# An mLSTM and bilinear kernel: the low words' top bits made on ACT instead of DVE, from the sixth weight stage on

## The chip, the cores and the metric

The kernel runs on one core of a Trainium2 chip. Its time is device time in microseconds (us), median of several runs. Engines are named as the profile names them: PE (matmul) and PEld (its weight loads), DVE, ACT, POOL, and SP, which here only issues DMAs.

## The reference

Inputs are float64. First a gated linear attention over 768 steps, for 4 batches and 8 heads of width 40:

```python
for t in range(S):
    m_new = np.maximum(f_gate[:, :, t] + m, i_gate[:, :, t])
    f_stab = np.exp(f_gate[:, :, t] + m - m_new)
    i_stab = np.exp(i_gate[:, :, t] - m_new)
    m = m_new
    C = f_stab[..., None, None] * C + i_stab[..., None, None] * np.einsum('bhd,bhe->bhde', vt, kt)
    n = f_stab[..., None] * n + i_stab[..., None] * kt
    h_tilde = np.einsum('bhde,bhe->bhd', C, qt)
    nq = np.einsum('bhd,bhd->bh', n, qt)[:, :, None]
    y[:, :, t] = sigmoid(o_gate[:, :, t]) * h_tilde / np.maximum(np.abs(nq), 1.0)
```

Then a bilinear layer on the 3072 tokens x 320 features: `out = ((x @ w_a) * (x @ w_b)) @ w_out`, with an inner width of 1536.

## The kernel before, in words

**Chunks and blocks.** A chunk is 128 steps of one batch (24 chunks, 8 heads each). Two or three chunks make a block of tokens (nine blocks; the first two have two chunks, 256 columns). For each block the bilinear layer (`moe_block`) runs over 12 slices ff of 128 inner columns: `up(ff)` makes two PSUM tiles pu (16 matmuls), ACT copies the first to g, DVE multiplies the second into it, ACT rounds the product to gh, POOL (later DVE) makes the rest gl, and two slices later `down(ff)` multiplies gh and gl with w_out into pd. While a block runs, the attention of the following chunks is woven in (`run_block`).

**Weights.** The weights come as 64-bit words by DMA (`fetch`, raw tiles), in 32 stages of 128 rows by 384 or 320 columns: for each three ff slices four stages of w_a and w_b, one that holds the last 64 rows of both, and three of w_out. Each stage is turned into float32 and split in two parts for PE:
- `high` (L342, ACT): the words' high halves, rescaled, go to a buffer `step` (four of them, in the qks tiles).
- `low` (L349, DVE): the words' low halves, as unsigned integers times 2^-29 and at most 7: the top three bits, into a buffer cw (four of them).
- `join` (L354, DVE): the high part shifted left by three, or'ed with the low bits, in cw.
- `lead_part` (L367, ACT): cw rounded to the leading part of w. `low_part` (L373, DVE): the rest.

Stages 0 to 4 are written out by hand in the opening. Stages 5 to 31 come from `weights()`, one step at each fourth PE instruction of block 0.

**Order.** The opening is in written order. In blocks 0 and 1 a list scheduler orders the instructions of every engine by its own timeline and costs; from block 2 on only ACT, DVE and POOL are ordered by it, PE and SP by hand. Each engine executes its queue strictly in the order built.

**Gates.** `later_gates` makes the decay tables: scans on DVE (L218, L228), a DMA to g_dram (L235) and back as gbc (L180), transposes on PE (ptg), an Exp on ACT into gtab (L263). From gtab POOL makes vw = v times its weight (L854), one buffer for all chunks, and PE's state update pU (L544) needs vw. POOL also masks gbc (L406) once the DMA has brought it back. `begin_e` makes the decay matrix of chunks 2 and 3 on PE (pE, in the same three PSUM buffers as pu) and ACT (Exp, L784). ACT's Exp and Sigmoid are in different tables, so that an ACT_TABLE_LOAD stands wherever they alternate.

Of the kernel before, what the change touches and what calls it, by code (L numbers as in the profile page):

```python
# [12 lines left out]
U32 = mybir.dt.uint32  # L13
I64 = mybir.dt.int64
AF = mybir.ActivationFunctionType
ALU = mybir.AluOpType
# [4 lines left out]
def kernel(  # L21
# [13 lines left out]
    nc = tc.nc  # L35
# [63 lines left out]
    x = ident[0:BH, 0:BH].rearrange("k (x j) -> k x j", j=2)  # L99
# [211 lines left out]
    NF0 = 5  # L311
# [25 lines left out]
    def high(x):  # L337
        raw, n, W = held[x]
        if W is None:
            held[x][2] = cpool.tile([P, WCH], F32, tag="cv", name="cw", bufs=CVB)[:, :n]  # L340
        hi = raw.bitcast(F32).rearrange("p (n w) -> p n w", w=2)[:, :, 1]
        nc.scalar.activation(  # L342
            step[x % len(step)][:, :n], hi, AF.Prelu, scale=2.0 ** -112, alpha=-(2.0 ** 32)
        )

    def low(x):
        raw, n, W = held[x]
        lo = raw.bitcast(U32).rearrange("p (n w) -> p n w", w=2)[:, :, 0]
        nc.vector.tensor_scalar(W.bitcast(U32), lo, 2.0 ** -29, 7.0, op0=ALU.mult, op1=ALU.min)  # L349

    def join(x):
        raw, n, W = held[x]
        wu, tu = W.bitcast(U32), step[x % len(step)][:, :n].bitcast(U32)
        nc.vector.scalar_tensor_tensor(  # L354
            wu, tu, 3, wu, op0=ALU.logical_shift_left, op1=ALU.bitwise_or
        )
# [6 lines left out]
    def lead_part(x):  # L363
        raw, n, W = held[x]
        w = ws[x] = rpool.tile([P, 2, n], F32R, tag=f"s{x}", name=f"w{x}")
        for rows, other, j, jl in parts(x):
            after["act"] = nc.scalar.copy(w[rows, j], W[rows]).ins  # L367

    def low_part(x):
        raw, n, W = held.pop(x)  # L370
        w = ws[x]
        for rows, other, j, jl in parts(x):
            after["dve"] = nc.vector.tensor_tensor(  # L373
                w[other, jl], W[rows], w[rows, j].bitcast(F32), op=ALU.subtract
            ).ins

    def weights():
        for x in range(NF0, len(stages) + 1):
            if x < len(stages):
                with tc.issue_after(start["act"]):  # L380
                    high(x)
                with tc.issue_after(start["dve"]):
                    low(x)
                join(x)
                yield x
            if x > NF0:
                ready[0] = x
                lead_part(x - 1)
                low_part(x - 1)
                yield x  # L390
        for x in qks2:
            for w in range(2):
                nc.gpsimd.memset(x[:, w, :, 3 * D:], 0.0)
# [502 lines left out]
    with tc.manual_schedule(engines={mybir.EngineType[x] for x in ("PE", "Activation", "DVE", "SP")}):  # L896
# [40 lines left out]
        high(0)  # L937
        run(E[0], 2)
        low(0)
        join(0)  # L940
        lead_part(0)
# [6 lines left out]
        run(S_[1])  # L948
        high(2)
        low(2)  # L950
        join(2)
        lead_part(2)
# [36 lines left out]
        for g in (*A, *E, *S_, *V, *F, *X):  # L989
            assert next(g, "end") == "end"  # L990
    conv = weights()

    def rest():
# [73 lines left out]
```

## Time and profile before

| | |
|---|---|
| median of 3 runs | 566.85 us (566.21 to 568.91) |
| profiled execution | 564.22 us, span 562.4 us |
| PE busy | 534.6 us, 95% of the span |
| DVE, ACT, POOL busy | 411.9, 221.3, 126.6 us |
| last weight stage done (L373) | 88.9 us after the span's start |

A row of a timeline gives start, duration, engine, line, operation, tiles and how many instructions it merges; in brackets stands the idle time of the engine before it and what ended it. Rows that follow each other closely overlap by about 0.1 us. A row of groups gives busy time and mean ns of one. PEclk is the clock that PE was granted.

### The profile page before, as it was taken

The page shows a single profiled execution, that of the slowest core. Times are in us where ns is not written, and L with a number is a line of the kernel's source. Part 1 is how long each engine was busy: PE and PEld are TensorE (multiplying, and loading weights), DVE is VectorE, ACT ScalarE, POOL GpSimd, SP SyncE. Part 2 cuts the span into 40 slices and gives each one's busy share as a digit, 9 for nine tenths or more (in the row PEclk, how much of TensorE's full clock was granted, in tenths as well). Part 3 has the DMA queues.
Part 4 walks back from the last instruction along what each step waited for, and adds up shares of the span by engine and source line. Part 5 has one row for each costly group of instructions (what it writes and reads, how often), then busy time and mean ns, then how long its engine had stood idle before and what let it go on. Part 6 is the DMA issues. An engine that isn't in the chain of part 4 may idle for free.

```text
span 562.4 us, 12436 instructions
## 1 busy us (share of the span) xinstructions
PE 534.6 (95%) x4810; PEld 505.9 (90%) x4810; DVE 411.9 (73%) x967; ACT 221.3 (39%) x530; POOL 126.6 (23%) x185
## 2 busy tenths in 40 slices
PE   9678799997999999999999999999999999899997
PEld 6576699997999989999899999899999999799997
DVE  6899976468879965978859995978859577744342
ACT  5677854344422642332632441541432515111111
POOL 2012245253331230332132231233030202100000
PEclk9587789999999999999999999999999999999999
DMA  9999513567956955677855654967544834200001
GB/s 172 300 273 303 110 38 89 117 95 160 153 135 105 167 119 76 146 142 158 139 119 119 120 108 106 190 121 155 89 122 75 139 76 114 35 1 24 2 0 36
DMA packets 198679, 66.77 MB, mean 119 GB/s; under 512 B 184252, under 2 KB 191900, under 8 KB 198620
## 3 DMA queue, kind: packets, MB, share of 16 engines
q1 hardware_dynamic: 198620, 65.98, 57.8%
q8 instruction: 38, 0.62, 0.5%
q14 instruction: 21, 0.17, 0.1%
HBM read 41.11 MB, written 5.97 MB: 84 GB/s over the span
## 4 chain that ended last, share of the span: by engine, by line
PE 68%; DVE 5%; DMA 5%; issue 4%; ACT 3%; SPq 2%; POOL 1%; POOLq 0%; ACTq 0%; DVEq 0%
PE pu L744 39%; PE pd L716 18%; PE pV L520 3%; PE pS L468 2%; PE pU L544 2%; DMA osig<-in_o_gate_dram 1%; ACT gbc L413 1%; PE pX L630 1%; PE pS L818 1%; PE pI L494 1%; PE pV L870 1%; DMA T<-qks 1%; SPq L160 1%; DMA gbc<-g_dram 1%; DMA qk<-in_q_dram 1%
## 5 line engine op out<-in xcount | busy, mean ns | idle before, releaser
L744 PE MATMUL pu<-xh,w 128*128 128x384 f32 (+1 forms) x1080 | 282.5, 328 | 3.9 <-DVE w L373 2.2
L744 PE MATMUL pu<-xl,w 128*128 128x384 f32 (+1 forms) x648 | 210.7, 327 | 1.0 <-DVE xl L636 1.0
L744 PEld LDWEIGHTS pu<-xh,w 128*128 128x128 f32 x1080 | 194.1, 192 | 7.1 <-DVE w L373 3.4
L716 PE MATMUL pd<-w,gh 128*128 128x320 f32 x576 | 132.8, 315 | 1.0 <-ACT gh L754 1.0
L744 PEld LDWEIGHTS pu<-xl,w 128*128 128x128 f32 x648 | 124.7, 193 | 2.0 <-DVE xl L636 1.3
L716 PEld LDWEIGHTS pd<-w,gh 128*128 128x128 f32 x576 | 97.9, 190 | 1.6 <-ACT gh L754 1.2
L752 DVE TENSOR_TENSOR g<-pu,g 128x384 f32<-128x384 f32 (+1 forms) x108 | 54.6, 505 | 56.7 <-PE pu L744 53.7
L716 PE MATMUL pd<-w,gl 128*128 128x320 f32 x288 | 89.2, 315 | 0.0
L751 ACT COPY g<-pu 128x384 f32<-128x384 f32 (+1 forms) x92 | 40.5, 440 | 114.4 <-PE pu L744 114.1
L413 ACT ACTIVATE gbc<-gbc,gtab 128x128 f32<-128x128 f32 x160 | 49.4, 389 | 23.8 <-POOL gbc L406 23.8
L455 POOL TENSOR_TENSOR vr<-va 128x336 f32<-128x336 f32 x18 | 14.0, 775 | 187.1 <-PE pV L520 176.6
L716 PEld LDWEIGHTS pd<-w,gl 128*128 128x128 f32 x288 | 53.8, 189 | 0.0
L756 DVE TENSOR_TENSOR gl<-g,gh 128x384 fp32r<-128x384 f32 (+1 forms) x92 | 50.3, 546 | 1.6
L754 DVE CAST gh<-g 128x384 fp32r<-128x384 f32 (+1 forms) x96 | 32.7, 341 | 1.6
L475 ACT CAST pb<-gbc 128x512 bf16<-128x512 f32 x36 | 22.2, 616 | 26.7 <-DVE gbc L473 26.6
L527 DVE TENSOR_TENSOR num<-pV,num 128x336 f32<-128x336 f32 x18 | 9.1, 504 | 29.9 <-PE pV L520 29.9
L406 POOL TENSOR_SCALAR_AFFINE_SELECT gbc<-gbc 128x1024 f32<-128x1024 f32 x20 | 23.7, 1185 | 18.9 <-DMA gbc<-g_dram 17.1
L562 ACT CAST cb<-cst 128x168 bf16<-128x168 f32 x18 | 6.0, 331 | 54.6 <-DMA gbc<-g_dram 26.7
L473 DVE TENSOR_TENSOR gbc<-pS,gbc 128x512 f32<-128x512 f32 x36 | 24.5, 680 | 3.6 <-PE pS L468 3.6
L520 PEld LDWEIGHTS <-pb 128*128 128x128 bf16 x576 | 23.1, 96 | 4.2 <-DVE pb L479 1.8
L607 POOL TENSOR_TENSOR osig<-osig,den 128x320 f32<-128x320 f32 x22 | 17.0, 771 | 43.8 <-DVE den L602 25.4
L431 ACT CAST qks<-qk 128x320 bf16<-128x320 f32 x36 | 16.1, 452 | 27.3 <-DMA T<-qks 12.4
(130 smaller groups left out, 814.1 us busy)
## 6 DMA issues: line engine op xcount, KB each, us to landing
gbc<-g_dram SPq DMA_DIRECT2D x20, 512.0 KB
qk<-in_q_dram SPq DMA_DIRECT2D x24, 160.0 KB
qk<-in_k_dram SPq DMA_DIRECT2D x24, 160.0 KB
va<-in_v_dram SPq DMA_DIRECT2D x24, 160.0 KB
osig<-in_o_gate_dram SPq DMA_DIRECT2D x24, 160.0 KB
raw<-in_moe_w_out_dram SPq DMA_DIRECT2D x12, 320.0 KB
out_dram<-o SPq DMA_DIRECT2D x24, 160.0 KB
raw<-in_moe_w_a_dram SPq DMA_DIRECT2D x8, 384.0 KB
```

The lines of the kernel that those rows point to most:

```text
L406: nc.gpsimd.affine_select(E, E, pattern=[[0, H], [1, P]], compare_op=ALU.is_ge, fill=-1e30, base=0, channel_multiplier=-1,)
L413: nc.scalar.activation(E[:, h], E[:, h], AF.Exp, bias=beta[:, h:h + 1])
L473: nc.vector.tensor_tensor(E, pS, E, op=ALU.mult)
L475: nc.scalar.copy(pb[:, 0], E)
L520: nc.tensor.matmul(pv[:, h], pb[i][:, h % HH, :], vb[j][:, h], start=(x == 0), stop=(x == len(terms) - 1),)
L607: (nc.vector if n < NS else nc.gpsimd).tensor_tensor(yv, yv, den.unsqueeze(2).broadcast_to([P, H, D]), op=ALU.mult)
L716: nc.tensor.matmul(pd[t][:, 0:DM], a[:, cols], w, start=(ff == 0 and first), stop=(ff == NF - 1 and last),)
L744: up_in = nc.tensor.matmul(acc[j], a, r, start=(x == 0), stop=(x == len(terms) - 1),).ins
L751: (nc.vector.tensor_copy if kb > 0 and ff in [1, 2] else nc.scalar.copy)(g, acc[0])
L752: nc.vector.tensor_tensor(g, acc[1], g, op=ALU.mult)
L754: (nc.vector.tensor_copy if kb > 0 else nc.scalar.copy)(gh, g)
L756: (nc.gpsimd if kb * 12 + ff < 16 else nc.vector).tensor_tensor(gl, g, gh.bitcast(F32), op=ALU.subtract)
```

## The change

From stage 5 on, `low` is one ACT instruction: a copy with a scale of 7.499 x 2^-32, rounded to an integer, that gives 0 to 7. The wait that holds these stages back until the opening is done now stands before both ACT parts and before `join`; `low` on DVE is gone from them.

```diff
     def low(x):
         raw, n, W = held[x]
         lo = raw.bitcast(U32).rearrange("p (n w) -> p n w", w=2)[:, :, 0]
-        nc.vector.tensor_scalar(W.bitcast(U32), lo, 2.0 ** -29, 7.0, op0=ALU.mult, op1=ALU.min)
+        if x < NF0:
+            nc.vector.tensor_scalar(W.bitcast(U32), lo, 2.0 ** -29, 7.0, op0=ALU.mult, op1=ALU.min)
+        else:
+            nc.scalar.activation(W.bitcast(U32), lo, AF.Copy, scale=7.499 * 2.0 ** -32)
...
                 with tc.issue_after(start["act"]):
                     high(x)
+                    low(x)
                 with tc.issue_after(start["dve"]):
-                    low(x)
-                join(x)
+                    join(x)
                 yield x
```

The lines after it move down by three (L406 is L409 in the changed kernel, L854 is L857); the new instruction is L352. The scheduler orders blocks 0 and 1 anew. Three places follow.

**POOL, where the state updates begin** (vw_634, vw_661 and vw_802 are the weighted v of chunks 0, 1 and 2; gbc_696 is chunk 4's gate table that comes by DMA). Before:

```order
L756 TENSOR_TENSOR gl_2_649<-g_2_608,gh_2_647 128x256
L854 TENSOR_TENSOR vw_634<-va_86,gtab 128x336
L756 TENSOR_TENSOR gl_3_783<-g_3_742,gh_3_781 128x256
L393 MEMSET qks_92 128x8x8 x2
L406 AFFINE_SELECT gbc_696<-gbc_696 128x1024
L854 TENSOR_TENSOR vw_661<-va_87,gtab 128x336
L854 TENSOR_TENSOR vw_802<-va_88,gtab 128x336
L756 TENSOR_TENSOR gl_4_864<-g_4_830,gh_4_862 128x256
```

In the change:

```order
L759 TENSOR_TENSOR gl_2_649<-g_2_608,gh_2_647 128x256
L857 TENSOR_TENSOR vw_634<-va_86,gtab 128x336
L857 TENSOR_TENSOR vw_661<-va_87,gtab 128x336
L759 TENSOR_TENSOR gl_3_783<-g_3_742,gh_3_781 128x256
L396 MEMSET qks_92 128x8x8 x2
L857 TENSOR_TENSOR vw_802<-va_88,gtab 128x336
L857 TENSOR_TENSOR vw_1050<-va_86,gtab 128x336
L759 TENSOR_TENSOR gl_4_864<-g_4_830,gh_4_862 128x256
L409 AFFINE_SELECT gbc_696<-gbc_696 128x1024
```

The mask of gbc_696, which waits for its DMA, stood ahead of vw_661; now three vw stand ahead of it.

**ACT, where chunk 2's decay matrix is made** (pE_0 and pE_1 are its halves, osig_159 the output gates, gh_0 the first rounded product). Before:

```order
L784 ACT_TABLE_LOAD
L784 ACTIVATE gbc_513<-pE_0_514 128x512
L367 CAST w_509<-cw 128x320
L342 ACTIVATE qks_89<-raw_180 128x384
L367 CAST w_560<-cw 128x320
L342 ACTIVATE qks_90<-raw_182 128x384
L784 ACTIVATE gbc_513<-pE_1_535 128x512
L167 ACT_TABLE_LOAD
L167 ACTIVATE osig_159<-osig_159 128x320
L367 CAST w_588<-cw 128x384
L342 ACTIVATE qks_89<-raw_184 128x384
L167 ACTIVATE osig_159<-osig_159 128x320
```

In the change:

```order
L342 ACTIVATE qks_90<-raw_182 128x384
L787 ACT_TABLE_LOAD
L787 ACTIVATE gbc_513<-pE_0_514 128x512
L167 ACT_TABLE_LOAD
L167 ACTIVATE osig_159<-osig_159 128x320
L787 ACT_TABLE_LOAD
L787 ACTIVATE gbc_513<-pE_1_535 128x512
L370 CAST w_588<-cw 128x384
L342 ACTIVATE qks_89<-raw_184 128x384
L167 ACT_TABLE_LOAD
L167 ACTIVATE osig_159<-osig_159 128x320
L757 CAST gh_0_502<-g_0_470 128x256
```

A sigmoid now stands between the two Exps and another behind them, with four table loads where there were two.

**ACT, where gtab is made** (w_686 is stage 12, g_3_742 the copy of slice 3's first PSUM tile). Before:

```order
L367 CAST w_686<-cw 64x384 x2
L342 ACTIVATE qks_89<-raw_198 128x384
L367 CAST w_723<-cw 128x320
L342 ACTIVATE qks_90<-raw_200 128x384
L751 COPY g_3_742<-pu_3_0_691 128x256
L263 ACT_TABLE_LOAD
L263 ACTIVATE gtab<-gtab 128x5x64
```

In the change:

```order
L370 CAST w_686<-cw 64x384 x2
L342 ACTIVATE qks_89<-raw_198 128x384
L352 ACTIVATE cw<-raw_190 128x320
L352 ACTIVATE cw<-raw_192 128x320
L352 ACTIVATE cw<-raw_194 128x320
L263 ACT_TABLE_LOAD
L263 ACTIVATE gtab<-gtab 128x5x64
L269 ACTIVATE dec<-pdec 128x64
L352 ACTIVATE cw<-raw_198 128x384
L754 COPY g_3_742<-pu_3_0_691 128x256
```

The copy g_3 stood ahead of the table load; now the table load, the Exp and four of the new instructions stand ahead of it.

## The prediction

> **What bounds the kernel now.** I read the page first, then the busy time by stretches, then the timelines of PE, POOL and ACT between 25 and 92 us, where stages 5 to 31 are converted.
>
> ```profile
> span 562.4 us, 12436 instructions
> PE 534.6 (95%) x4810; PEld 505.9 (90%) x4810; DVE 411.9 (73%) x967; ACT 221.3 (39%) x530; POOL 126.6 (23%) x185
> PEclk9587789999999999999999999999999999999999
> ```
>
> PE is busy for 95% of the span, and its clock is below full only in the first six of the 40 slices (84 us). After that nothing can be gained but PE's small gaps; an edit in the weight stages counts by how far it moves PE's queue there. By stretches:
>
> ```profile
> core 0: us, PE busy (x) PEld busy (x) DVE busy (x) ACT busy (x) POOL busy (x), PEclk, DMA share, GB/s
> 26.00:62.00 36.00, 27.13 (x196) 23.06 (x194) 34.01 (x74) 26.52 (x61) 7.10 (x12) 0.81 0.99 255
> 62.00:74.00 12.00, 12.00 (x81) 11.42 (x82) 9.13 (x21) 10.47 (x29) 3.32 (x5) 0.57 0.49 82
> 74.00:88.00 14.00, 14.00 (x125) 13.26 (x124) 13.06 (x27) 7.86 (x22) 6.73 (x12) 1.00 0.19 42
> 25.50:87.20 61.70, 52.83 (x394) 47.43 (x394) 55.72 (x118) 44.86 (x111) 17.14 (x28) 0.80 0.72 174
> 58.80:62.00 3.20, 0.01 (x2) 0.01 (x2) 2.53 (x6) 1.20 (x5) 1.98 (x2) 1.00 0.34 69
> ```
>
> From 26 to 62 us DVE is full (34.0 of 36) and PE has 8.9 us of idle time; ACT has 9.5 free. The largest single gap of PE is 58.8 to 62.0, and behind it PE has work without a break but a clock of 0.57 for 12 us. What ended the gap, on PE and on POOL:
>
> ```profile
> 52.67 0.58 PE L744 MATMUL pu<-xh,w 128*128 128x256 f32 x1
> 56.69 0.67 PE L544 MATMUL pU<-vw,qk 128*64 128x42 f32 x16
> 61.99 0.67 PE L544 MATMUL pU<-vw,qk 128*64 128x42 f32 x16 [3.19 <-POOL vw L854]
> 76.13 1.16 PE L818 MATMUL pS<-T,T 40*128 40x128 f32 x8
> 88.26 0.28 PE L744 MATMUL pu<-xl,w 128*128 128x256 f32 x1
> ```
>
> ```profile
> 51.90 0.83 POOL L854 TENSOR_TENSOR vw<-va,gtab 128x336 f32<-128x336 f32 x1 [7.82 <-ACT gtab L263]
> 56.05 0.35 POOL L393 MEMSET qks<- 128x64 bf16 x2 [1.16 <-DMA g_dram<-qks]
> 59.95 1.20 POOL L406 TENSOR_SCALAR_AFFINE_SELECT gbc<-gbc 128x1024 f32<-128x1024 f32 x1 [3.56 <-DMA gbc<-g_dram]
> 61.12 0.81 POOL L854 TENSOR_TENSOR vw<-va,gtab 128x336 f32<-128x336 f32 x1
> ```
>
> The vw of chunk 1 could have been made when PE had used chunk 0's (the pU at 56.69, over by 57.4), but POOL stood at the mask of gbc until its DMA landed at 59.9. So this gap is one of POOL's order, not of DVE or ACT.
>
> **The change part by part.** *The instructions.* 27 `low` go from DVE (15 of 384 columns, 12 of 320) and 27 come to ACT:
>
> ```profile
> L349 DVE TENSOR_SCALAR cw<-raw 128x384 uint32<-128x384 uint32 x20 | 7.3, 365 | 0.1
> L349 DVE TENSOR_SCALAR cw<-raw 128x320 uint32<-128x320 uint32 x12 | 4.9, 412 | 0.1
> L342 ACT ACTIVATE qks<-raw 128x384 f32<-128x384 f32 x20 | 10.9, 552 | 0.5 <-DMA raw<-in_moe_w_a_dram 0.5
> L342 ACT ACTIVATE qks<-raw 128x320 f32<-128x320 f32 x12 | 5.8, 499 | 0.0
> L367 ACT CAST w<-cw 128x384 fp32r<-128x384 f32 x16 | 8.2, 510 | 4.8 <-DVE cw L354 4.8
> L367 ACT CAST w<-cw 128x320 fp32r<-128x320 f32 x12 | 5.4, 452 | 2.7 <-DVE cw L354 2.7
> ```
>
> DVE is relieved of 15 x 0.365 + 12 x 0.412 = 10.4 us. No row shows ACT with integers. The nearest are L342, which reads the same raw words with the same stride, and L367, the cheaper copy. I take 0.53 and 0.48, between them; queued closely, ACT's instructions start 0.1 us sooner than these durations say:
>
> ```profile
> 34.56 0.56 ACT L342 ACTIVATE qks<-raw 128x384 f32<-128x384 f32 x1
> 35.02 0.45 ACT L367 CAST w<-cw 128x320 fp32r<-128x320 f32 x1
> 35.37 0.56 ACT L342 ACTIVATE qks<-raw 128x384 f32<-128x384 f32 x1
> ```
>
> (0.46 and 0.35 from start to start.) So a `low` costs ACT 0.43 or 0.38, and all of them 15 x 0.43 + 12 x 0.38 = 11.0 us. Bounds: the cheaper cast throughout, 10.4; twice my value, 22, if integers halved ACT's rate. The new order also has two more table loads in this stretch:
>
> ```profile
> 29.34 0.46 ACT L367 CAST w<-cw 128x320 fp32r<-128x320 f32 x1 [0.91 <-DVE cw L354]
> 31.12 0.59 ACT L808 COPY T<-pT 128x512 f32<-128x512 f32 x1 [0.87 <-PE pT L805]
> 33.72 0.60 ACT L784 ACTIVATE gbc<-pE 128x512 f32<-128x512 f32 x1 [0.71 <-PE pE L783]
> 36.43 1.28 ACT L167 ACT_TABLE_LOAD   x1
> 37.72 0.47 ACT L167 ACTIVATE osig<-osig 128x320 f32<-128x320 f32 x1
> 39.31 0.69 ACT L754 CAST gh<-g 128x256 fp32r<-128x256 f32 x2
> 49.67 0.37 ACT L751 COPY g<-pu 128x256 f32<-128x256 f32 x1 [0.23 <-PE pu L744]
> 50.06 1.28 ACT L263 ACT_TABLE_LOAD   x1
> 51.35 0.47 ACT L263 ACTIVATE gtab<-gtab 128x320 f32<-128x320 f32 x1
> ```
>
> A load takes 1.29 from its start to the next instruction's (36.43 to 37.72), two take 2.6. ACT's work in 25.5 to 87.2 goes from 44.9 to 44.9 + 11.0 + 2.6 = 58.5 of 61.7 us: ACT becomes the fullest engine there, and DVE falls to about 45.
>
> [...]
>
> *First place: gh_0, late.* Before gh_0 stand four new copies (3 x 0.38 + 0.43 = 1.6) and the two loads (2.6), 4.2 us, of which ACT's idle time there (0.91 + 0.87 + 0.71 = 2.5) takes 2.5. With the second half of the decay matrix, now behind three loads, freeing PE's PSUM buffer at about 38.8, I get gh_0 at 41.3 instead of 39.31: PE's first `down` 2.0 us late. It makes half of it good, since in 44 to 50 it waited for weights (w_611 to w_686) that come no later than before: `join` no longer stands behind `low` on a full DVE.
>
> *Second place: g_3, late.* Three copies, a load, the Exp, its small neighbour and another copy (3 x 0.38 + 1.29 + 0.38 + 0.13 + 0.43 = 3.4) stand before g_3. ACT reaches them at about 47.9 (gh_0 ends its slot at 41.6; behind it four `low`, a g, two gh, five casts of leads and four `high` are 6.3 us with no gap), so g_3 is over at 51.6, not 50.0. Its PSUM buffer holds up the second half of chunk 3's decay matrix and the state update behind it. With both of these (2 us) behind 51.6, PE comes to slice 4 (52.67 before) at about 53.7: **1.0 us late**, the first place included. The Exp itself starts at 50.3, 1.0 us earlier (51.35), and with it vw of chunk 0.
>
> *Third place: POOL.* vw of chunk 1 now follows chunk 0's at once (about 53.4 to 54.1, when PE has used the first). The third vw waits for the g_dram DMA, which the memset waits for (56.05 above), and is over at 58.1; PE comes to it at 59. The mask of gbc stands behind, and nobody needs it before ACT's Exps of chunk 4 at about 68. So the gap of **3.2 us** is gone. And PE's clock: 12 us at 0.57 from 62 on are 12 x 0.43 = **5.2 us** of lost pulses after that gap. Without it I take the clock as full. By this PE is over with the second half of pS of chunk 3 (76.13 + 1.16 = 77.3 before) at about 70.
>
> *The tail.* From there ACT must not let PE starve. From g_3 at 51.6 on, its queue up to the leading part of stage 28 (w_1197) is 28.7 us long, each instruction at its row's duration less 0.1, so that stage comes at about 80:
>
> ```profile
> 81.43 1.05 ACT L367 CAST w<-cw 64x384 fp32r<-64x384 f32 x2 [0.98 <-DVE cw L354]
> 83.80 2.28 DVE L373 TENSOR_TENSOR w<-cw,w 64x384 fp32r<-64x384 f32 x3
> ```
>
> PE used this stage at 88.26, and if it is 7 us ahead wants it at 81 to 82. It fits, with 1 to 2 us to spare and no more.
>
> *Sum:* -3.2 - 5.2 + 1.0 = -7.4, of which I give 1.0 back for small waits on a full ACT: **-6.4 us**. Behind 90 us PE has no gaps for 25 us and the shift is carried on. The profiled execution takes 564.22 us, 1.8 more than its span, and would take 557.8; it lies 2.6 below the median shown, so I predict 566.85 - 6.4 = **560.4 us**.
>
> **The rivals.** *ACT starves PE* (slower). For: 58.5 of 61.7 us leave 3.2, and `lead_part` waits at ACT's head for `join`, while now `join` waits for ACT:
>
> ```profile
> ACT w L367 <- DVE cw L354: 7.4, 9, 1.5
> DVE w L373 <- ACT w L367: 2.3, 3, 1.0
> ```
>
> If ACT keeps the 16.8 us of idle time that it has in this stretch, its last leads come 13.6 us later: stage 28's at 81.43 + 13.6 + 1.0 = 96.0, its rest by 98. PE wanted it at 88.26: 9 to 10 us lost, 576. It decides once ACT idles more than about 5 us between 48 and 80. Against it: most of those 7.4 us came from a full DVE, which is relieved; the same mechanism takes over if a `low` costs twice what I took.
>
> *The gap goes, the slow clock stays* (no change). The new waits of PE, 38 to 41.7 and 48.5 to 51.6 by my working, may cost it the clock as the old one did. Then -3.2 + 1.0 = -2.2 is left: 564.6. For: the low clock of the third to sixth slice came with such gaps. Against: it rose again at 74 under steady work, and the work from 53 on is steady.
>
> [...] The trace shows 0.57 after an idle 3.2. [...]
>
> *DVE's relief is the gain, and more* (faster still). If weights reach PE earlier all along, the rest of PE's gaps of 26 to 62 go too: at most 8.9 - 3.2 = 5.7 us more, 555. Against: ACT cannot deliver faster than 1.3 us a stage at best (0.46 + 0.43 + 0.41), and its table loads lie there.
>
> **How the numbers follow.** Forecast 0.48 (556 to 563); slow clock stays 0.22 (563 to 567); starving 0.20 (570 to 577); more gain 0.10 (553 to 556). Range 554 to 572, which leaves out the worst of starving. About 0.5% (2.8 us) can be told from no change. Faster: the forecast, the last case, and a little of the second, 0.60; same: the rest of the second and some of the third, 0.21; slower 0.19.
>
> **What would show it.** In the changed profile: no wait of PE at pU for POOL's vw near 57 to 62, clock 1.0 from about 60; pS of chunk 3 over near 70; gh_0 at 41, g_3 at 51; the new copies at 0.48 to 0.55 us; the last L376 before 86. The forecast is wrong if PE waits for w L376 or L370 after 70 us, if ACT idles over 5 us between 48 and 80, or if the clock is 0.5 in 60 to 70.

## The result: 566.87 to 552.14 us

| | before | the change |
|---|---|---|
| median | 566.87 us (566.21 to 568.91) | 552.14 us (551.70 to 555.06) |
| profiled execution | 564.22 us, span 562.4 | 555.06 us, span 553.3 |
| mean granted clock, profiled | 0.969 | 0.975 |
| PE, DVE, ACT busy | 534.6, 411.9, 221.3 us | 529.7, 407.9, 233.8 us |

The ratio is 0.9747, with an interval of 0.9715 to 0.978: 14.7 us by the medians, 9.1 between the two profiled executions. The profile shows before in an execution quicker than all its other runs on record and the change in the slowest of its four. The forecast was 6.4 us.

The page of the changed kernel:

```profile
span 553.3 us, 12427 instructions
PE 529.7 (96%) x4810; PEld 504.1 (91%) x4810; DVE 407.9 (74%) x940; ACT 233.8 (42%) x559; POOL 126.5 (23%) x185
PEclk9687899999999999999999999999999999999999
```

Its busy time by stretches, the first four as in the prediction, the fifth where time went that the prediction didn't speak of:

```profile
core 0: us, PE busy (x) PEld busy (x) DVE busy (x) ACT busy (x) POOL busy (x), PEclk, DMA share, GB/s
26.00:62.00 36.00, 28.55 (x239) 26.03 (x239) 29.59 (x54) 35.73 (x79) 8.03 (x13) 0.84 0.97 248
62.00:74.00 12.00, 12.00 (x83) 11.16 (x82) 8.82 (x18) 11.79 (x35) 5.67 (x7) 0.72 0.60 120
74.00:88.00 14.00, 14.00 (x124) 13.45 (x123) 11.24 (x25) 9.85 (x26) 5.75 (x8) 1.00 0.30 76
25.50:87.20 61.70, 54.25 (x437) 50.34 (x437) 48.90 (x94) 57.48 (x137) 18.88 (x27) 0.85 0.75 185
115.00:136.00 21.00, 19.74 (x230) 18.73 (x229) 17.89 (x42) 7.38 (x22) 8.60 (x11) 1.00 0.77 142
```

The same last stretch before:

```profile
115.00:136.00 21.00, 17.62 (x170) 16.41 (x169) 14.77 (x37) 8.60 (x28) 9.75 (x14) 1.00 0.63 116
```

ACT is full from 26 to 62 (35.73 of 36) and DVE is not (29.59, before 34.01). PE gets 43 more instructions done in that time. From 115 to 136 PE works 2.1 us more than before and gets 60 more done.

PE's rows where it waits, with the state updates pU and the decay scores pS, in the changed kernel:

```profile
38.82 0.38 PE L747 MATMUL pu<-xh,w 128*128 128x256 f32 x1 [0.71 <-ACT gbc L787]
...
41.75 1.43 PE L719 MATMUL pd<-w,gh 128*128 128x320 f32 x4 [1.72 <-ACT gh L757]
...
52.35 0.22 PE L784 MATMUL pE<-cx 96*128 96x128 bf16 x1 [1.11 <-ACT g L754]
...
52.90 0.67 PE L547 MATMUL pU<-vw,qk 128*64 128x42 f32 x16
...
55.95 0.85 PE L719 MATMUL pd<-w,gh 128*128 128x320 f32 x4 [1.04 <-ACT gh L757]
...
56.73 0.67 PE L547 MATMUL pU<-vw,qk 128*64 128x42 f32 x16
...
59.27 0.67 PE L547 MATMUL pU<-vw,qk 128*64 128x42 f32 x16
...
72.63 1.16 PE L821 MATMUL pS<-T,T 40*128 40x128 f32 x8
...
106.57 1.71 PE L821 MATMUL pS<-T,T 40*128 40x128 f32 x16
...
125.46 0.57 PE L497 MATMUL pI<-cx,T 120*128 120x42 bf16 x16
```

The gap of 3.2 us ahead of the second pU is gone. The shift of a PE instruction between the two profiles is its start now less its start before. For the pS of 76.13 it is -3.5; for the pS of 111.27 and the pI of 134.22 (rows below) it is -4.7 and -8.8. So four more microseconds come between 111 and 134, where before had this on PE:

```profile
102.68 0.32 PE L544 MATMUL pU<-vw,qk 128*64 128x42 f32 x4
...
108.85 0.32 PE L544 MATMUL pU<-vw,qk 128*64 128x42 f32 x4
...
109.53 0.31 PE L544 MATMUL pU<-vw,qk 128*64 128x42 f32 x2
...
111.27 1.49 PE L818 MATMUL pS<-T,T 40*128 40x128 f32 x16
...
126.94 0.22 PE L468 MATMUL pS<-T,T 120*128 120x128 bf16 x1 [0.44 <-DMA T<-qks]
...
128.65 0.56 PE L468 MATMUL pS<-T,T 120*128 120x128 bf16 x7 [1.49 <-DMA T<-qks]
...
134.22 0.56 PE L494 MATMUL pI<-cx,T 120*128 120x42 bf16 x16 [1.04 <-DVE gbc L473]
```

and this on ACT and DVE:

```profile
127.69 0.46 ACT L431 CAST qks<-qk 128x320 bf16<-128x320 f32 x1 [5.51 <-DMA T<-qks]
```

```profile
110.62 0.32 DVE L555 TENSOR_TENSOR cst<-pU,cst 128x168 f32<-128x168 f32 x1
...
128.18 0.24 DVE L442 COPY qks<-qks 128x320 bf16<-128x320 bf16 x1 [5.68 <-ACT qks L431]
```

The state update of chunk 4 (pU_1441) stands on PE in pieces: three of its eight heads ahead of slice 8, five between the slices of the next block (the rows of 102.68 to 109.53). Only then comes its addition to the state (110.62), and behind it in DVE's queue the preparation of chunk 6. That chunk's transposing DMA is late; ACT waits 5.51 us for it, DVE 5.68 behind ACT, and PE in three places (the rows of 126.94, 128.65 and 134.22). In the change all eight heads stand together at slice 8, and the addition on DVE starts at 95.14:

```profile
95.14 0.33 DVE L558 TENSOR_TENSOR cst<-pU,cst 128x168 f32<-128x168 f32 x1
```

### The profile page after: what moved, and what is told of

Same layout as the page of the kernel before. It is cut to its first block, busy times and chain, and to the rows that moved or that the text cites. A ratio compares the mean times of both kernels' runs of the same rounds, so it can differ in the third digit from the quotient of the medians.

```text
span 553.3 us, 12427 instructions
## 1 busy us (share of the span) xinstructions
PE 529.7 (96%) x4810; PEld 504.1 (91%) x4810; DVE 407.9 (74%) x940; ACT 233.8 (42%) x559; POOL 126.5 (23%) x185
## 4 chain that ended last, share of the span: by engine, by line
PE 74%; ACT 10%; DVE 5%; DMA 5%; issue 4%; SPq 2%; POOL 1%; POOLq 0%; ACTq 0%; DVEq 0%
PE pu L747 40%; PE pd L719 20%; PE pV L523 3%; DMA osig<-in_o_gate_dram 2%; PE pS L471 2%; PE pU L547 2%; ACT qks L342 1%; ACT L167 1%; ACT w L370 1%; PE pS L821 1%; PE pX L633 1%; PE pV L873 1%; SPq L160 1%; ACT cw L352 1%; ACT gbc L416 1%
## 5 line engine op out<-in xcount | busy, mean ns | idle before, releaser
L757 DVE CAST gh<-g 128x384 fp32r<-128x384 f32 (+1 forms) x96 | 34.2, 356 | 1.6
L409 POOL TENSOR_SCALAR_AFFINE_SELECT gbc<-gbc 128x1024 f32<-128x1024 f32 x20 | 23.6, 1182 | 14.6 <-DMA gbc<-g_dram 12.3
L523 PE MATMUL pV<-va,pb 128*128 128x42 bf16 x288 | 25.0, 183 | 1.6 <-DVE pb L482 1.6
```

Of the source, the lines that this page charges most:

```text
L409: nc.gpsimd.affine_select(E, E, pattern=[[0, H], [1, P]], compare_op=ALU.is_ge, fill=-1e30, base=0, channel_multiplier=-1,)
L523: nc.tensor.matmul(pv[:, h], pb[i][:, h % HH, :], vb[j][:, h], start=(x == 0), stop=(x == len(terms) - 1),)
L757: (nc.vector.tensor_copy if kb > 0 else nc.scalar.copy)(gh, g)
```

## The experiments

The change does three things at once: `low` moves to ACT, DVE is relieved, and the scheduler puts all queues of blocks 0 and 1 in another order. To part them, most kernels below hold every engine's queue in a given order by a table of instruction numbers; each instruction is queued behind the one ahead of it in its row, without any wait:

```diff
+    made = {x.name: x for x in nc.cur_bb.bb.instructions}
+    for row in PIN:
+        row = [f"I-{x}" for x in row]
+        for x, y in zip(row, row[1:]):
+            tc.add_manual_dep(
+                made[y], x, mybir.DependencyInfo(mybir.DependencyClass.NoSync, mybir.DependencyReason.DATA),
+                reason="pin",
+            )
+
+PIN = [
...
```

Below, such a table is shown by the queue that it makes. Ratios are to the kernel before, on the same chip.

### The instruction without the order, the order without the instruction

`low` on ACT right behind `high`, all else in the order of before:

```diff
-            nc.vector.tensor_scalar(W.bitcast(U32), lo, 2.0 ** -29, 7.0, op0=ALU.mult, op1=ALU.min)
+            nc.scalar.activation(W.bitcast(U32), lo, AF.Copy, scale=7.499 * 2.0 ** -32)
...
+PIN = [
...
```

> The copy that makes the low words' bits stands on ACT, each right behind the high part of its stage, but every engine's queue is otherwise held in the order of before (the mask of gbc ahead of the vw of chunk 1; chunk 6's preparation behind T5). Theory A, the gain lies in the order: PE still waits some 3 us for that vw near 62, the stall of 4.2 us between 121 and 136 stays, and the time is 563 to 570. Theory B, the gain lies in DVE's relief of 10.4 us: weights come earlier, the waits for w L376 between 44 and 50 go, and the time is 552 to 558.

571.68 us, ratio 1.0092 (1.0071 to 1.0114): slower by 4.6, above both expected ranges. `low` on DVE, and all else in the change's order:

```diff
+            nc.vector.tensor_scalar(W.bitcast(U32), lo, 2.0 ** -29, 7.0, op0=ALU.mult, op1=ALU.min)
-            nc.scalar.activation(W.bitcast(U32), lo, AF.Copy, scale=7.499 * 2.0 ** -32)
...
+PIN = [
...
```

> The low bits are made on DVE as before, each right ahead of its join, but every engine's queue is otherwise held in the order of the change. Theory A: the wait at the state update and the stall at 121 to 136 are gone, and the time is 552 to 558. Theory B: DVE is as full as before (10.4 us more than in the change between 26 and 88), weights are late, and the time is 564 to 572.

558.12 us, ratio 0.9844 (0.9807 to 0.9882): faster by 8.9 with no instruction moved between engines. PE's four longest waits in the first kernel (ACT's `low`, old order) from 40 us on:

```profile
43.02 1.43 PE L719 MATMUL pd<-w,gh 128*128 128x320 f32 x4 [2.83 <-ACT gh L757]
...
55.39 0.22 PE L784 MATMUL pE<-cx 96*128 96x128 bf16 x1 [1.79 <-ACT g L754]
...
60.69 1.43 PE L719 MATMUL pd<-w,gh 128*128 128x320 f32 x4 [1.79 <-ACT gh L757]
...
68.27 0.67 PE L547 MATMUL pU<-vw,qk 128*64 128x42 f32 x16 [1.78 <-ACT cst L552]
```

All these waits are for ACT's rounded products and copies, which stand behind the new `low`: the starving rival, in an order where it can happen. In the second kernel (DVE's `low`, new order), the stretch of the weights and PE's two waits for DVE:

```profile
26.00:62.00 36.00, 25.71 (x226) 22.69 (x224) 34.23 (x66) 28.95 (x61) 7.28 (x13) 0.90 1.01 255
```

```profile
55.33 0.38 PE L744 MATMUL pu<-xh,w 128*128 128x256 f32 x1 [2.39 <-DVE g L752]
...
62.99 0.38 PE L744 MATMUL pu<-xh,w 128*128 128x256 f32 x1 [2.62 <-DVE g L752]
```

DVE is full again (34.23 of 36) and PE waits for its products. So the move of `low` costs 4.6 in the old order and brings 558.12 - 552.14 = 6.0 in the new one (5.5 by the ratios, some 3 to 8 by their intervals); the order brings 8.9 with `low` on DVE and 571.68 - 552.14 = 19.5 with it on ACT.

### POOL's mask alone

Before, with the mask of chunk 4's gate table behind the vw of chunks 1 and 2, POOL's order of the change at that place:

```diff
-L406 AFFINE_SELECT gbc_696<-gbc_696 128x1024
 L854 TENSOR_TENSOR vw_661<-va_87,gtab 128x336
 L854 TENSOR_TENSOR vw_802<-va_88,gtab 128x336
+L406 AFFINE_SELECT gbc_696<-gbc_696 128x1024
```

> The kernel before in its own order, with one instruction moved on POOL: the mask of gbc of chunk 4 stands behind the vw of chunks 1 and 2. Theory A as the prediction had it: the 3.2 us go and the slow clock of 62 to 74 with them, -6 to -8, 559 to 561. If the slow clock stays: -2 to -3.5, 563 to 565. Theory B: 566 to 567.5, since the state update then waits for something else.

564.63 us, ratio 0.9963 (0.9943 to 0.9982): less than the gap was worth. POOL and PE in it:

```profile
53.30 0.75 POOL L854 TENSOR_TENSOR vw<-va,gtab 128x336 f32<-128x336 f32 x1 [8.12 <-ACT gtab L263]
...
58.94 3.19 POOL L854 TENSOR_TENSOR vw<-va,gtab 128x336 f32<-128x336 f32 x1 [2.44 <-PE pU L544]
```

```profile
62.18 0.67 PE L544 MATMUL pU<-vw,qk 128*64 128x42 f32 x16 [1.44 <-POOL vw L854]
...
68.79 1.16 PE L818 MATMUL pS<-T,T 40*128 40x128 f32 x8 [2.62 <-DVE T L808]
```

The vw that was no longer held by the mask took 3.19 us in place of 0.75, while DVE ran without a break, mostly `join` and `low_part`, so that PE still waited 1.44. Then ACT stood 4.3 us at chunk 4's Exps, which need the mask that is now later, with leads behind them; DVE stood 3.6 for these, and PE waited 2.62 more. What made that vw slow the rows don't show, and it was seen once: in the change's profile the same instruction (at 53.71), beside a DVE busy for 0.92 us of it, took 1.07.

The same kernel with the eight Exps of chunk 4 behind gh_4:

```diff
 L549 COPY cst_93<-pU_636 128x168
-L413 ACTIVATE gbc_696<-gbc_696,gtab 128x128 x2
 L367 CAST w_957<-cw 64x384 x2
-L413 ACTIVATE gbc_696<-gbc_696,gtab 128x128 x6
 L367 CAST w_981<-cw 128x320
...
 L754 CAST gh_4_862<-g_4_830 128x256
+L413 ACTIVATE gbc_696<-gbc_696,gtab 128x128 x8
```

> The kernel before in its own order, with the mask of chunk 4's gbc behind the vw of chunks 1 and 2 as in the experiment before, and in addition ACT's eight Exps that need this mask behind gh_4, so that ACT does not stand before them. The prediction's first term alone: the waits of PE at pU and at chunk 3's pS go and the half clock behind them, 559 to 561. If the half clock stays or another wait comes up: 562.5 to 565.

565.52 us, ratio 0.995 (0.9917 to 0.9984): above both expected ranges. In its profile the wait at pU is gone and the clock is full from 62 to 74, but it is lower ahead of that (0.74 over 26 to 62, before 0.81), and PE waits 1.88 for chunk 3's q at 57.8. The shift is -3.0 at 74 us and -3.5 later. So the wait and the half clock behind it, taken away together, brought 1 to 5 us in this order by the interval, and not the 8.4 that the prediction added up for them.

### The half clock behind the gap

Before, with twelve matmuls of no use in the gap ahead of chunk 1's pU (they write into its PSUM tile and are overwritten):

```diff
+        for _ in range(12 if n == 1 else 0):
+            nc.tensor.matmul(
+                pU.rearrange("p (x t) -> p x t", x=4), identb, mask.unsqueeze(1).broadcast_to([P, 4, P]),
+                start=True, stop=True,
+            )
         for h in range(H):
```

> The kernel before in its own order, with 12 matmuls without use (128x512 bf16, some 0.21 us each at full clock) on PE ahead of the state update of chunk 1, where PE waits 3.2 us; their result is overwritten. The wait stays, but PE works in it. If the idle time is what brings the half clock of 63.5 to 73.8, as the prediction had it: that stretch goes, -3 to -5, 562 to 565, and the mean clock rises by 0.006 to 0.009. If the half clock comes from something else: 566 to 569 and the same clock.

The stretch behind the gap in it:

```profile
62.00:74.00 12.00, 11.98 (x112) 10.39 (x111) 10.92 (x24) 11.27 (x33) 5.02 (x7) 1.00 0.55 83
```

The clock is full, where before had 0.57, and PE gets 112 instructions done in place of 81. The twelve matmuls themselves took 2.75 us, 0.23 each. 563.80 us, ratio 0.993 (0.9899 to 0.9962): 4.0 us (2 to 6 by the interval) come from the clock, with the wait itself left in. The prediction had 5.2.

### The late stall

Before's order up to 96 us and the change's from there on:

```diff
+L544 MATMUL pU_1441<-vw_1420,qk_81 64x42 x5
 L744 MATMUL pu_8_1_1127<-xh_406,w_867 128x256
...
-L716 MATMUL pd_0_446<-w_981,gh_6_1011 128x320 x2
-L716 MATMUL pd_0_446<-w_981,gl_6_1013 128x320
 L805 MATMUL pT_1_1035<-ident,qk_81 128x128 x4
...
```

> The kernel before, its queues in the order of before up to about 96 us and in the order of the change from there on; the low bits on DVE. Theory A: only the stall at 121 to 136 goes, -3.5 to -4.5, 562 to 563.5. Theory B: 566 to 567.5.

566.21 us, ratio 0.9989 (0.9957 to 1.002): no difference. The stall of 126 to 134 was gone, but where the two orders meet PE waited 0.99 (at 96.6), and the clock was halved for 3.4 us there: the shift is +3.3 by 104 us and -1.1 behind the place of the stall. The other way round, the change's order up to 79 us and before's from there on:

```diff
+L547 MATMUL pU_1441<-vw_1420,qk_81 64x42 x3
 L747 MATMUL pu_8_0_1126<-xh_406,w_833 128x256
...
-L547 MATMUL pU_1441<-vw_1420,qk_81 64x42 x8
 L747 MATMUL pu_8_1_1127<-xh_406,w_867 128x256
...
```

> The change, its queues in its own order up to about 79 us and in the order of before from there on (chunk 6's preparation behind T5 again); the low bits on ACT. If the stall of PE between 121 and 136 is worth its 4.2 us, it comes back and the time is 555.5 to 557. If all of the gain is made before 79 us, 551.5 to 553.

563.87 us, ratio 0.9929 (0.9898 to 0.996): 11.7 lost of the change's gain (10.3 by the ratios), more than both expectations. The stall is back:

```profile
125.54 0.22 PE L471 MATMUL pS<-T,T 120*128 120x128 bf16 x1 [0.63 <-DMA T<-qks]
...
127.04 0.56 PE L471 MATMUL pS<-T,T 120*128 120x128 bf16 x7 [1.29 <-DMA T<-qks]
```

Against the change's profile, 7.3 us quicker, 3.7 come at 124 to 134, and 3.3 stand there by 100 us, behind the seam, where PE waited 0.96 and 1.46 and the clock was halved from 85 to 92. Cutting an order in two makes a seam with costs of its own, so a smaller edit was tried: before, with chunk 4's state update put together on PE, and its addition and chunk 6's preparation moved up behind it on DVE (their two neighbours on ACT and POOL likewise):

```diff
-L544 MATMUL pU_1441<-vw_1420,qk_81 64x42 x3
+L544 MATMUL pU_1441<-vw_1420,qk_81 64x42 x8
...
-L544 MATMUL pU_1441<-vw_1420,qk_81 64x42 x2
...
 L551 TENSOR_TENSOR cst_93<-cst_93,dec 128x168
+L555 TENSOR_TENSOR cst_93<-pU_1441,cst_93 128x168
...
+L435 TENSOR_TENSOR r_0_1577<-qk_80,qks_89 128x320
```

> The kernel before in its own order, low bits on DVE, with one thing of the change's order: chunk 4's state update. Five of its eight matmuls, which stand about 103 and 109 us, come to the first three at slice 8 (some 83 us), and what waits for them (the addition into cst, its rounding, chunk 6's preparation on DVE and POOL) comes ahead of T5. If the stall of 4.2 us between 121 and 136 is due to this late state update: it goes, -3.5 to -4.5 against before, 563 to 564.5. If not: 566.5 to 569.

563.58 us, ratio 0.9931 (0.991 to 0.9952): 3.9 us by this alone. The shift against before's profile changes by 3.8 us between 101 and 131, which is where the stall was.

### Is ACT the bound of the change?

Each of ACT's `low` done twice, so that ACT has some 11 us more work (13.9 by the durations):

```diff
-            nc.scalar.activation(W.bitcast(U32), lo, AF.Copy, scale=7.499 * 2.0 ** -32)
+            for _ in range(2):
+                nc.scalar.activation(W.bitcast(U32), lo, AF.Copy, scale=7.499 * 2.0 ** -32)
```

> The change in its own order, with each of the 27 low copies on ACT done twice: 11 to 12 us more work for ACT. If ACT's queue sets PE's pace up to the last weight stage (the rival of starving, 9 to 10 us lost): 560 to 566. If ACT has slack from about 72 us on: its lateness stays under 5 us, 554 to 557.

563.44 us, ratio 0.9931 (0.9905 to 0.9957): 11.3 slower than the change (10.4 by the ratios). PE waits for ACT, here in the profile of its slowest execution (570.62 us at a clock of 0.955; the others took 562.58 to 564.17):

```profile
40.72 0.38 PE L748 MATMUL pu<-xh,w 128*128 128x256 f32 x1 [2.47 <-ACT gbc L788]
...
43.65 1.44 PE L720 MATMUL pd<-w,gh 128*128 128x320 f32 x4 [1.46 <-ACT gh L758]
...
58.47 0.22 PE L785 MATMUL pE<-cx 96*128 96x128 bf16 x1 [3.69 <-ACT g L755]
```

So more work on ACT lengthens the weight stages of the change. That it does so one for one is not shown: some 4 us of the 11 are clock by an estimate, since the other executions had 0.966 to 0.973 where the change has 0.975 to 0.978, and this share of the pulses, (0.9765 - 0.97) x 563, is 3.7 us. With a `low` of twice the price, 3.9 us of the gain are left.

If ACT is the bound, its table loads are dear (1.28 us each in the profiles of before and of the change). The change's order has two sigmoids among the Exps. They were moved behind gh_3, and in another kernel behind the copy of chunk 1's state, which makes two table loads fewer:

```diff
 L787 ACTIVATE gbc_513<-pE_0_514 128x512
-L167 ACT_TABLE_LOAD
-L167 ACTIVATE osig_159<-osig_159 128x320
-L787 ACT_TABLE_LOAD
 L787 ACTIVATE gbc_513<-pE_1_535 128x512
...
-L167 ACT_TABLE_LOAD
-L167 ACTIVATE osig_159<-osig_159 128x320
 L757 CAST gh_0_502<-g_0_470 128x256
...
-L263 ACT_TABLE_LOAD
 L263 ACTIVATE gtab<-gtab 128x5x64
...
 L757 CAST gh_3_781<-g_3_742 128x256
+L167 ACT_TABLE_LOAD
+L167 ACTIVATE osig_159<-osig_159 128x320 x2
...
+L787 ACT_TABLE_LOAD
 L787 ACTIVATE gbc_727<-pE_0_728 128x512
```

> The change in its own order, but for the two sigmoids that stand between the Exps of chunk 2's decay matrix and ahead of gh_0: they come behind gh_3, so that three table loads and two sigmoids (4.7 us) leave the stretch of ACT ahead of gh_0, and two loads (2.6 us) leave the program. If ACT's queue is what holds PE up between 38 and 56 us: PE's waits for L787 (0.71) and for gh (1.72) go, and with them some of the half clock, 547 to 550. If weights or their DMA come too late anyway: 551 to 553.

> The change with its two sigmoids behind the second copy of cst (about 59 us) in place of behind gh_3. If the wait of 1.5 us for cst that the earlier place brought is all that ate its gain: 549 to 551.5. If PE then waits for the transfer of qk (1.4 us, seen at 57.7 there) and the half clock comes back: 552 to 554.5.

554.34 us, ratio 0.9772 (0.9723 to 0.982), and 554.86 us, ratio 0.9774 (0.9752 to 0.9796): no gain on the change. The waits for the Exp and for gh at 38 to 42 us are gone, and PE, earlier by these, waits for another thing, as in the second of the two:

```profile
42.74 0.36 PE L747 MATMUL pu<-xh,w 128*128 128x256 f32 x1 [1.22 <-ACT w L370]
...
56.58 1.11 PE L808 MATMUL pT<-ident,qk 128*128 128x128 f32 x4 [2.81 <-DMA qk<-in_q_dram]
```

That pT, chunk 3's first transpose, waits for a DMA that brings q. With it put behind the second half of slice 4:

```diff
-L808 MATMUL pT_0_773<-ident,qk_80 128x128 x4
 L747 MATMUL pu_4_1_810<-xh_406,w_611 128x256
...
+L808 MATMUL pT_0_773<-ident,qk_80 128x128 x4
 L547 MATMUL pU_837<-vw_802,qk_82 64x42 x8
```

> The change with its two sigmoids behind the second copy of cst, and in addition the four transpositions of chunk 3's q, where PE then stood 2.8 us for the transfer of qk (56.6), behind the second half of slice 4. If that wait is all that took the sigmoids' gain: it is filled with slice 4's work, -2 to -4 against the change, 548.5 to 550.5. If PE then waits at slice 5 for weights from a full ACT: 552 to 554.

557.46 us, ratio 0.9834 (0.9803 to 0.9865), from 551.55 at a granted clock of 0.984 to 559.81 at 0.963: a program that can be as quick as the change and mostly isn't. Its six executions are the slower the lower their clock.

### The change again, and with its waits filled

The change once more, with its own order written down as a table and nothing else edited:

> The change once more, its own order written down: nothing is changed, so 551.7 to 555. Its second profile shows how far one execution differs from another: if the half clock's windows make the difference, their number between 20 and 80 us differs by one for each 1.7 us.

552.83 us, ratio 0.9757 (0.9705 to 0.9809). In this profile the stretch behind the old gap has a full clock, where the first profile of the change had 0.72:

```profile
62.00:74.00 12.00, 12.00 (x106) 11.33 (x105) 9.97 (x23) 12.00 (x36) 5.67 (x7) 1.00 0.59 104
```

In the profiles of before and of the change the clock is either full or half, and up to the last microsecond of the span the half clock comes in stretches of 3.4 us or of two, three or five times that (17.1, 6.8 and 10.2 us before, 10.2, 3.4, 6.8 and 6.8 in the change): 1.7 us of lost pulses for each 3.4. The repeat's shift against before is some -6.7 at 91 us. Then the change with 19 matmuls of no use at three of its waits (overwritten, as above):

```diff
+        for _ in range(6 if n == 1 else 0):
+            nc.tensor.matmul(pX.rearrange("p (x t) -> p x t", x=4), identb, mask.unsqueeze(1).broadcast_to([P, 4, P]), start=True, stop=True)
...
+            for _ in range(7 if (kb, ff) == (0, 0) else 0):
+                nc.tensor.matmul(pd[0].rearrange("p (x t) -> p x t", x=4), identb, mask.unsqueeze(1).broadcast_to([P, 4, P]), start=True, stop=True)
...
+            for _ in range(6 if (n, j) == (2, 0) else 0):
+                nc.tensor.matmul(pT.rearrange("p (x t) -> p x t", x=4), identb, mask.unsqueeze(1).broadcast_to([P, 4, P]), start=True, stop=True)
```

> The change in its own order, with matmuls without use (128x512 bf16, results overwritten) in three of PE's own waits: 6 ahead of the second transposition of the opening (wait of 2.7 us near 18), 6 ahead of the transposition of chunk 2's q (2.5 us near 28), 7 ahead of the first down (1.7 us near 40). If the half clock that the change still has (20 to 27 us) follows these waits: mean clock up from 0.975 to 0.982 or more, -2 to -4, 548 to 550.5. If it does not: the clock stays, 552 to 554, or later where the fillers delay PE.

553.39 us, ratio 0.9737 (0.9713 to 0.9762): the granted clock rises to between 0.981 and 0.988, and the time stays. PE comes earlier to the places where it needs ACT, and waits longer there, for the Exp 2.14 (0.71 in the change, 1.09 in its repeat):

```profile
38.66 0.52 PE L751 MATMUL pu<-xh,w 128*128 128x256 f32 x1 [2.14 <-ACT gbc L791]
```

Ahead of this wait PE's slow pulses had cost nothing. The last kernel joins the late sigmoids, the late pT and twelve of these matmuls:

> The change with the sigmoids and chunk 3's first transposition later as in the run before, and 12 matmuls without use in PE's two waits ahead of 30 us (6 ahead of the second transposition of the opening, 6 ahead of chunk 2's). In the run before, one and the same program took 551.6 at a clock of 0.984 and 559.8 at 0.963. If the idle time ahead of 30 us decides which of these it is: clock 0.98 or more in nearly all, 548.5 to 551. If not: 551.5 to 560 again.

The ratio is 0.9782 (0.9736 to 0.9829). Five of its six executions took 552.34 to 556.40 us at clocks of 0.978 to 0.985, the sixth 564.07 at 0.967: the higher clock brought no gain on the change here either. No version beat the change.

## Why the prediction was wrong

**What held.** The gap at pU went, by the order of POOL as worked out: second vw at 53.71 (forecast 53.4), third pU at 59.27 (59). ACT's rounded gh_0 came at 41.31 (41.3), g_3 was over at 52.3 (51.6), and slice 4 began at 53.7 (53.7). ACT's work from 25.5 to 87.2 is 57.48 us (58.5), with `low` at 0.564 and 0.493 (0.53 and 0.48):

```profile
L352 ACT ACTIVATE cw<-raw 128x384 uint32<-128x384 uint32 x15 | 8.1, 564 | 0.0
...
L352 ACT ACTIVATE cw<-raw 128x320 uint32<-128x320 uint32 x12 | 5.8, 493 | 0.0
```

DVE's is 48.9 (45). ACT didn't starve PE, though it became the fullest engine. The last `low_part` starts at 90.85, later than before and not before 86 as was written, and PE doesn't wait for it; that sign said nothing.

**What held in one of two executions.** PE was to be over with chunk 3's pS near 70, a shift of -7.3. In the change's profile it was over at 73.8, a shift of -3.5, because the clock was half from 65.0 to 71.8 though the gap ahead was gone:

```profile
65.00:71.80 6.80, 6.80 (x40) 6.38 (x41) 5.98 (x14) 6.61 (x21) 3.97 (x5) 0.50 0.56 90
```

In the repeat the clock was full there, and pS was over at 70.0:

```profile
68.87 1.16 PE L821 MATMUL pS<-T,T 40*128 40x128 f32 x8
```

So the sum for the weight stages came out as forecast in the repeat, and in the other the slow clock stayed for 6.8 us, the second rival's case, but with no wait of PE over 0.3 us for 9 us ahead of it, so that new waits were its cause is not shown.

**First failing step: "Behind 90 us PE has no gaps for 25 us and the shift is carried on."** It is carried on to 111 us (-4.7 in the change's profile, -6.9 in the repeat), and then four microseconds are added in both, because a stall of before ends. The row of waits at 126 to 134 stood in the trace of before; the prediction read the order only where the weights are, though the scheduler orders two whole blocks anew, and put this term at nothing. The edit of that one state update brings 3.9 us.

**Second failing step: "it lies 2.6 below the median shown, so I predict 566.85 - 6.4".** The prediction came to 557.8 us for an execution like the profiled one and added 2.6 to reach the median, as if the change's median lay as far above. It doesn't: the change's other runs took 551.70 to 552.28, and the repeat's profiled 553.12 lies 0.3 above its median. Without these 2.6 and with the stall's 4.1 (the shift goes from -4.7 to -8.8), the same sum gives 553.7.

Part of the 2.6 is clock. If the clock is either full or half in every execution, as it is in the two profiles, the mean granted clock gives the time at half clock: (1 - 0.969) x 2 x 562.4 = 34.9 us in the profiled execution before. Over the 92 runs of before beside these experiments its median is 0.960, so 45 us; the change has 0.975 to 0.981 with its repeat, 21 to 28 us. Of those 92 runs the ten with 0.966 or more have a median of 566.3 us, the eleven under 0.956 one of 570.5. But the mean clock doesn't explain everything: of the change's runs, 555.06 and 552.28 both had 0.975. The clock term itself, "12 us at 0.57 from 62 on are 12 x 0.43 = 5.2 us", took the half clock of one execution as if it were the kernel's. Filling the gap gave 4.0 of it, so its size is near for this stretch; but the change's profile has half clock there without the gap, and in the order of before the gap's wait and clock together brought only 2.8.

**The third rival, more gain by DVE's relief,** had 0.10 and a range of 553 to 556, just above the median that came. Its reason did not show: PE's other gaps between 26 and 62 were to go, but they were 8.9 - 3.2 = 5.7 us before and are 36 - 28.55 = 7.4 in the change. The waits for weights went, and waits for ACT came. DVE's relief counts all the same, by 5.5 us between `low` on DVE and on ACT in the new order.

The parts measured one by one are the gap 2.8, its clock 4.0, the state update 3.9, `low` off a full DVE 5.5: 16.2, where the whole is 14.7. That these come near each other is no check: they were measured in different orders, and the kernel without the gap already has what its going did to the clock.

**What stays open:** what sets how much half clock one execution of a program gets, and with it how the gain divides between the gap, its clock and DVE's relief. The kernel with the late sigmoids and the late pT varied over 8 us with its clock, and filling two of its waits didn't bring it below the change.

## What to carry to other kernels

Where a scheduler orders the queues, an edit of one instruction is an edit of every queue: compare the order over its whole reach and look for the stalls that go or come far from the edit, since here the order alone brought 8.9 us and the moved instruction alone cost 4.6. Relief of an engine at 34 of 36 us can pay even if the engine that takes the work becomes as full, but here only in an order made for it: the same move cost 4.6 in the old order and brought 5.5 in the new one. And a clock term is to be taken from many executions' mean clock, not from the one that was profiled.

## What was not expected of the hardware

**Half clock without a gap ahead.** In the repeat of the change, three stretches of 3.4 us, in which PE is busy throughout; its last wait before them was one of 0.2 us at 59.8:

```profile
77.60:81.00 3.40, 3.40 (x29) 3.09 (x27) 3.33 (x11) 3.35 (x10) 1.86 (x4) 1.00 0.14 34
81.00:84.40 3.40, 3.40 (x15) 3.40 (x16) 3.31 (x6) 2.07 (x7) 2.52 (x3) 0.50 1.07 244
84.40:87.80 3.40, 3.40 (x26) 3.09 (x26) 3.21 (x6) 2.28 (x9) 2.10 (x7) 1.00 0.46 64
```

The clock is halved for just 3.4 us, and PE does 15 instructions in place of 26 to 29. The full clock behind the filled gap (1.00 in place of 0.57) speaks for idle time as a cause; these rows have none ahead of the slow one, so it isn't shown to be the only cause. Nor is it by the half clock of 65.0 to 71.8 in the change's first profile, which has no wait of PE over 0.3 us ahead of it since 56.

**Half clock that costs nothing.** With filled waits the change's mean granted clock was 0.981 to 0.988, where it is 0.975 to 0.981 in the change's eight runs, and the time stayed: PE's wait for ACT's Exp took up what it had gained.

**A POOL instruction of 0.75 us took 3.19 once** beside a DVE without a break, and 1.07 in the change beside a DVE busy for 0.92 of it.
